# The last two token groups of an attention and MLP-mixer kernel as the column halves of one Strassen product

## The chip, the cores and the metric

The kernel runs on one core of a Trainium2 chip. A core has TensorE (PE; it multiplies a loaded 128 x 128 weight block with up to 512 columns and adds into PSUM), VectorE (DVE), ScalarE (ACT), GpSimd (POOL) and SyncE (SP, whose queue here only issues DMAs). The engines run side by side and meet at semaphores. The metric is device time in microseconds; the runs shown are of one launch each.

## The reference, cut to what matters

Linear attention over 8 batches, 8 heads, 576 tokens and 64 channels a head, and then an MLP mixer over the attention's result x (8 x 576 x 512):

```python
kv = einsum('bhsd,bhse->bhde', softmax_over_tokens(k), v)
x  = einsum('bhsd,bhde->bhse', softmax_over_channels(q), kv)   # heads side by side: 512 channels
h  = relu(x.T @ w_tok1) @ w_tok2          # tokens mix: 576 -> 256 -> 576
u  = x + h.T
h2 = relu(u @ w_ch1) @ w_ch2              # channels mix: 512 -> 1536 -> 512
return u + h2
```

The last two products are most of the work, and the change is there. Below they are ch1 and ch2.

## The kernel before

*Numbers.* The matrix products of the mixer take each float32 operand as a high and a low part of a type that TensorE reads in one pass (F32R), and form three of the four part products: high x high, low x high, high x low. So "one product" of 128 x 128 blocks is always three matmuls. `split` (L128) makes the parts: ACT casts the high one, DVE subtracts it for the low one.

*Units and groups.* The first part of the kernel treats 32 units, a batch and a pair of heads each (`load_unit`, `softmax_k`, `softmax_q`, and the stages in `pe_stages`, L685). A unit's last stage, `stage_u` (L440), writes u transposed (channels in partitions, tokens in columns) into `uT[g]`, high and low. The 4608 tokens are cut into nine groups of 512, counted g = 0 to 8; three buffers hold u for them in turn. The hidden 1536 channels are twelve blocks f of 128, the weights of ch1 and ch2 stay in SBUF as such blocks (`c1_row`, `c2_row`).

*Groups 0 to 2* run ch1 plainly (`ch1`, L472): 12 matmuls of 512 columns for each f into a bank of `ps_h`, then relu and the low part. ch2 (L634) takes such an f and adds 4 x 3 matmuls of 512 columns into four banks of `ps_o`, which `out_end` (L646) adds to u and writes.

*Groups 3 to 8* run ch1 by Strassen's scheme in Winograd's form: 2 x 2 blocks, seven products in place of eight. The 2 x 2 blocks are two f (a pair p = f // 2) by two halves of the 512 input channels, and the two halves of the group's 512 columns. `pair_a` (L599) forms the products P1, P6, P5 and P7, `pair_b` (L615) P2, P3 and P4; each `product` (L580) is 6 matmuls of 256 columns. The DVE adds at L607, L611, L612, L620 and L624 join them into both f's hidden values, and L629 and L630 make relu and the low part for ch2, which stays plain. The sums of data that the products need come from `data_sums` (L568) over the row sums u = high + low (`row_sum`, L562, on POOL or DVE).

*Where the weights come from.* The seven weight operands of a pair (blocks, and sums of blocks) are stored to DRAM once: `keep_blocks` (L495) and `keep_sums` (L503), six pairs each, at steps around the start of group 2. `load_product` (L542) loads one operand of 256 KB at a time into a ring of eight slots, one after each product used. All these DMAs are in SP's queue, in order. The sums pass through the two `stg` buffers, which also hold the row sums of even groups (`rows_of`, L551) until their output is written.

*The order.* `steps` (L761) lists (group, f); n0 = 24 is the step at which group 2 begins, and each later group has 12 steps. `put(at, fn)` hangs unit work, stored sums, row sums and data sums on steps or half steps; ch2 runs one f behind ch1 (`pend`). The units of a batch are hung on the steps of earlier groups, the last of them two steps ahead of group 7. The framework then makes each engine's instruction list by simulating the program, the earlier in the program first among what is ready, and puts in the waits. What an engine does is in that fixed order on the chip.

## Time and profile before

| | |
|---|---|
| median of 3 runs | 810.22 us (808.62 to 810.96) |
| the profiled execution's own time | 805.34 us |
| its span, first to last instruction | 803.5 us |
| granted TensorE clock | 1.00 of full speed |
| PE busy | 778.6 us, 5112 matmuls |
| DVE busy | 606.8 us, 1195 instructions |
| ACT busy | 380.2 us, 908 instructions |
| POOL busy | 113.1 us, 88 instructions |
| DMA | 148.09 MB, mean 184 GB/s |

In the profile's rows "L642 PE MATMUL ps_o<-h,c2h 128*128 128x512 f32 x672 | 225.1, 396" reads: line 642 of the kernel, engine, operation, what is written from what, shapes, how many, busy microseconds, and the mean nanoseconds of one. Matmuls overlap each other in the pipeline, so a matmul's 396 ns is not its share of the time: that is the distance from one start to the next. Behind the second bar stands the time for which the engine had been idle, and what ended that. "c" is a pair's hidden values, "th" and "tl" are the data sums' parts, "ring" the weight operands, "h" the operand of ch2. Groups 7 and 8 have no unit work beside them.

### The profile page before, as it was taken

Reading aid. Unit: us, or ns where it says so; the run is one execution under the profiler, and the core shown is the slowest. Engines: PE = TensorE matmul, PEld = TensorE weight load, DVE = VectorE, ACT = ScalarE, POOL = GpSimd, SP = SyncE. Lnnn points to the kernel's source line nnn. Section 1 sums busy time; section 2 is a strip of 40 time slices with the busy share of each in tenths; the row PEclk is TensorE's granted clock in tenths of the full one; section 3 lists DMA queues with packets and bytes.
Section 4 is the critical chain, followed back from the end, with each engine's and each line's share of the span. In section 5 each row is a group of like instructions: output and inputs, shape, how many; then the busy total and the mean of one; then the engine's idle time right before and its main releaser. Section 6 shows DMA issues by size and latency. Waiting matters only on the chain.

```text
span 803.5 us, 13913 instructions
## 1 busy us (share of the span) xinstructions
PE 778.6 (97%) x5112; PEld 688.9 (86%) x5112; DVE 606.8 (76%) x1195; ACT 380.2 (47%) x908; POOL 113.1 (14%) x88
## 2 busy tenths in 40 slices
PE   3899999989999999999999999999999999999998
PEld 2688888778888888999999899988999999999996
DVE  7989998999889766987797788887896556436333
ACT  4776433465664555655555455445655531122110
POOL 0000000101211331222112222112112201100000
PEclk9999999999999999999999999999999999999999
DMA  9754842315767742666657666766565446556651
GB/s 302 220 153 153 293 148 93 114 60 190 250 236 259 224 144 66 221 208 197 201 181 244 194 203 175 232 196 195 169 189 184 142 144 206 188 169 204 204 170 52
DMA packets 113922, 148.09 MB, mean 184 GB/s; under 512 B 48832, under 2 KB 60736, under 8 KB 113856
## 3 DMA queue, kind: packets, MB, share of 16 engines
q1 hardware_dynamic: 107520, 135.16, 53.9%
q10 hardware_dynamic: 6336, 12.06, 4.0%
q8 instruction: 40, 0.66, 0.3%
q14 instruction: 26, 0.21, 0.1%
HBM read 123.60 MB, written 23.59 MB: 183 GB/s over the span
## 4 chain that ended last, share of the span: by engine, by line
PE 68%; DVE 13%; issue 9%; DMA 5%; ACT 3%; POOL 2%; SPq 0%; DVEq 0%; POOLq 0%; ACTq 0%
PE ps_o L642 26%; PE ps_h L593 19%; PE ps_h L457 6%; PE ps_h L480 5%; PE ps_h L415 4%; DMA q_t<-in_q 4%; PE ps_h L353 2%; PE ps_o L457 1%; PE ps_h L423 1%; DVE st L322 1%; DVE q_t L323 1%; DVE q_t L401 1%; DVE q_t L336 1%; PE ps_o L415 1%; POOL ql L131 1%
## 5 line engine op out<-in xcount | busy, mean ns | idle before, releaser
L642 PE MATMUL ps_o<-h,c2h 128*128 128x512 f32 x672 | 225.1, 396 | 2.4 <-ACT h L483 2.4
L642 PEld LDWEIGHTS ps_o<-h,c2h 128*128 128x128 f32 x672 | 125.5, 188 | 27.2 <-ACT h L483 3.3
L642 PE MATMUL ps_o<-h,c2l 128*128 128x512 f32 x336 | 131.1, 393 | 0.0
L593 PE MATMUL ps_h<-th,ring 128*128 128x256 f32 x576 | 107.1, 283 | 0.7 <-DVE c L624 0.7
L593 PEld LDWEIGHTS ps_h<-th,ring 128*128 128x128 f32 x576 | 89.7, 191 | 0.9 <-DVE c L624 0.9
L593 PE MATMUL ps_h<-uh,ring 128*128 128x256 f32 x432 | 81.7, 282 | 0.0
L593 PE MATMUL ps_h<-tl,ring 128*128 128x256 f32 x288 | 81.4, 283 | 0.0
L593 PEld LDWEIGHTS ps_h<-uh,ring 128*128 128x128 f32 x432 | 70.4, 190 | 4.0 <-issue 0.4
L401 ACT COPY q_t<-cv_s 32x160 f32<-32x160 f32 (+1 forms) x232 | 71.8, 310 | 3.2 <-DVE cv_s L391 0.3
L314 POOL TENSOR_TENSOR k_t<-k_t,dg 128x640 f32<-128x640 f32 x24 | 41.2, 1718 | 222.9 <-ACT dg L313 214.8
L642 PEld LDWEIGHTS ps_o<-h,c2l 128*128 128x128 f32 x336 | 63.4, 189 | 10.4
L131 POOL TENSOR_TENSOR ql<-q_t,qh 128x640 fp32r<-128x640 f32 x24 | 39.4, 1642 | 178.6 <-DMA kt_t<-in_kt 100.9
L593 PE MATMUL ps_h<-ul,ring 128*128 128x256 f32 x216 | 61.0, 282 | 0.0
L629 ACT ACTIVATE h<-c 128x512 fp32r<-128x512 f32 x48 | 28.8, 624 | 60.0 <-DVE c L624 60.0
L480 PE MATMUL ps_h<-uh,c1l 128*128 128x512 f32 x144 | 56.2, 390 | 0.0
L480 PE MATMUL ps_h<-ul,c1h 128*128 128x512 f32 x144 | 56.2, 390 | 0.0
L480 PE MATMUL ps_h<-uh,c1h 128*128 128x512 f32 x144 | 56.1, 392 | 0.0
L593 PEld LDWEIGHTS ps_h<-tl,ring 128*128 128x128 f32 x288 | 55.2, 192 | 0.0
L332 ACT ACTIVATE q_t<-q_t 128x640 f32<-128x640 f32 x32 | 23.6, 739 | 51.1 <-DVE q_t L323 37.5
L464 ACT CAST uh<-ps_h 128x320 fp32r<-128x320 f32 (+4 forms) x76 | 24.7, 335 | 45.9 <-PE ps_h L457 34.3
L322 DVE TENSOR_REDUCE st<-q_t 128x10 f32<-128x640 f32 x32 | 26.2, 818 | 23.7 <-DMA q_t<-in_q 23.4
L593 PEld LDWEIGHTS ps_h<-ul,ring 128*128 128x128 f32 x216 | 41.0, 190 | 0.1
(196 smaller groups left out, 1758.4 us busy)
## 6 DMA issues: line engine op xcount, KB each, us to landing
ring<-w SPq DMA_DIRECT2D x252, 256.0 KB, 3.3
kt_t<-in_kt SPq DMA_DIRECT2D x32, 320.0 KB, 3.3
q_t<-in_q SPq DMA_DIRECT2D x32, 320.0 KB, 3.4
v_t<-in_v SPq DMA_DIRECT2D x32, 320.0 KB, 4.4
stg_w<-in_w SPq DMA_DIRECT2D x18, 512.0 KB, 6.2
k_t<-in_k SPq DMA_DIRECT2D x24, 320.0 KB, 4.8
w<-stg SPq DMA_DIRECT2D x12, 512.0 KB, 3.9
stg<-in_w SPq DMA_DIRECT2D x10, 512.0 KB, 5.1
```

Of the source, the lines that this page charges most:

```text
L131: lo_eng.tensor_tensor(lo, src, f32(hi), op=ALU.subtract)
L314: nc.gpsimd.tensor_tensor(kx, kx, dg.unsqueeze(1).broadcast_to([P, C1, P]), op=ALU.subtract)
L322: nc.vector.tensor_reduce(st[:, 0, :], qt, axis=AX.X, op=ALU.max)
L332: nc.scalar.activation(qc, qc, AF.Exp)
L401: eng(qx[ys, 0:n, xs], turned[xs, 0:n, ys])
L415: nc.tensor.matmul(y[:, 0:TOK], a, w, start=(i == 0), stop=(i == len(mm) - 1))
L457: nc.tensor.matmul(t[:, 0:N], a, w, start=(i == 0), stop=(i == len(mm) - 1))
L464: nc.scalar.copy(uh, src).ins,
L480: nc.tensor.matmul(t, a[:, n, :], w, start=(i == 0), stop=(i == 3 * NJ - 1))
L593: nc.tensor.matmul(t[:, cols], a, b[:, n], start=(i == 0), stop=(i == 5))
L629: nc.scalar.activation(hh, c[:, r], AF.Relu)
L642: m = nc.tensor.matmul(o, a[:, cs], w, start=(first and i == 0), stop=(last and i == 2))
```

## The change

Groups 7 and 8 (GA and GB) leave the step loop, and `both_groups` does them after it, together.

ch1: the two column halves of the 2 x 2 blocks are now group 7 and group 8, so each of the seven products of a pair is 6 matmuls of 512 columns for both groups. The data sums for that are made by `wide_sums` and `wide_split` on the last steps of group 6, from group 7's row sums and, for group 8, sums of its own in tiles of the finished units (`wide_rows`, on POOL). Their parts go into T, where group 6 has used its own, and into the buffer of u that group 6 leaves. The first pair takes its products in another order (`FIRST`), so that the operands that are made last are used last.

ch2: it is done by the same scheme. The 2 x 2 blocks are the two halves of a pair's f in the rows, the two halves of the 512 output channels, and the two groups as columns. Seven products over six pairs, each 6 matmuls of 512 columns; a product of all pairs is summed in two PSUM banks, then joined to the outputs by adds on DVE, ACT and POOL. The weight operands are stored to DRAM by `keep_out` (blocks) and `keep_out_sums` (sums), six times, at the steps in `KEEP`: two in group 2 and four in group 5. The hidden values of all pairs stay in SBUF; `operand` makes the parts of one data operand at a time, up to twelve ahead, and has POOL form the differences that later operands need.

The ring has eight slots as before up to group 6, and six for the joint part. The pools of the main part are closed ahead of it (`main_pools`), and its tiles take their place.

```diff
+    KEEP = (5.5, 7.5, 37, 38.5, 40, 41.5)
+    AHEAD = 12
...
-    scratch_w = {}
+    scratch_w, scratch_v = {}, {}
...
+    def keep_out(p):
+        scratch_v[p] = dpool.tile([P, 7, 2, 2 * P], F32, name=f"v{p}")
+        with behind(loaded):
+            for x, (w0, w1) in enumerate(zip(c2_row(2 * p), c2_row(2 * p + 1))):
+                nc.sync.dma_start(scratch_v[p][:, P1, x, :], f32(w0[:, 0 : 2 * P]))
+                nc.sync.dma_start(scratch_v[p][:, P2 : P4 + 1, x, :], f32(w1).rearrange("p (k m) -> p k m", k=2))
+    def keep_out_sums(p):
+        hi = stg.tile([P, CW, 2], U32, name="stg").rearrange("p n w -> p (n w)").bitcast(F32R)
+        lo = stg.tile([P, CW, 2], U32, name="stg").rearrange("p n w -> p (n w)").bitcast(F32R)
+        a = f32(hi).rearrange("p (f m) -> p f m", f=2)
+        (wh, wl), i = c2[2 * p]
+        nc.gpsimd.tensor_tensor(a, f32(wh[:, i : i + 2]), f32(wl[:, i : i + 2]), op=ALU.add)
+        s = f32(lo).rearrange("p (k m) -> p k m", k=4)
+        (a11, a21), (a12, a22) = ([a[:, f, x * 2 * P : (x + 1) * 2 * P] for x in range(2)] for f in range(2))
+        nc.vector.tensor_tensor(s[:, 0], a21, a22, op=ALU.add)
+        nc.vector.tensor_tensor(s[:, 1], s[:, 0], a11, op=ALU.subtract)
+        nc.vector.tensor_tensor(s[:, 2], a11, a21, op=ALU.subtract)
+        nc.vector.tensor_tensor(s[:, 3], a12, s[:, 1], op=ALU.subtract)
+        split(hi, lo, f32(lo), nc.vector)
+        for x, w in enumerate((hi, lo)):
+            nc.sync.dma_start(scratch_v[p][:, P5 : P3 + 1, x, :], f32(w).rearrange("p (k m) -> p k m", k=4))
...
     def stage_pair_pools(f0):
...
-            pool = ctx.enter_context(tc.tile_pool(name="pairs_b", bufs=1, reuse_waits="tile"))
+            pool = main_pools.enter_context(tc.tile_pool(name="pairs_b", bufs=1, reuse_waits="tile"))
...
-    loads = [(p, e) for g in range(G_S, NG) for p in range(NP) for e in (P1, P6, P5, P7, P2, P3, P4)]
-    asked = [0]
+    TURN = (P1, P6, P5, P7, P2, P3, P4)
+    FIRST = (P1, P5, P2, P3, P6, P7, P4)
+    GA, GB = NG - 2, NG - 1
+    turn_of = [FIRST] + [TURN] * (NP - 1)
+    loads = [(scratch_w, p, e) for g in range(G_S, GA) for p in range(NP) for e in TURN]
+    n_main = len(loads)
+    loads += [(scratch_w, p, e) for p in range(NP) for e in turn_of[p]]
+    loads += [(scratch_v, p, e) for e in TURN for p in range(NP)]
+    slot_of = [i % 8 if i < n_main else (i - n_main) % 6 for i in range(len(loads))]
+    after, to_load, last_in = {}, [], {}
+    for i, x in enumerate(slot_of):
+        (after.setdefault(last_in[x], []) if x in last_in else to_load).append(i)
+        last_in[x] = i
+    def load_at_place(i):
+        where, p, e = loads[i]
+        nc.sync.dma_start(f32(ring[slot_of[i]].rearrange("p n m -> p (n m)")), where[p][:, e].rearrange("p x m -> p (x m)"))
     def load_product():
-        i = asked[0]
-        if i < len(loads):
-            p, e = loads[i]
-            nc.sync.dma_start(f32(ring[i % 8].rearrange("p n m -> p (n m)")), scratch_w[p][:, e].rearrange("p x m -> p (x m)"))
-            asked[0] += 1
+        load_at_place(to_load.pop(0))
+    at_product, at_h = [0], [0]
+    def next_weights():
+        w = ring[slot_of[at_product[0]]]
+        at_product[0] += 1
+        return w
+    def weights_used():
+        for i in after.get(at_product[0] - 1, ()):
+            load_at_place(i)
     rows = {}
...
-    at_product, at_h = [0], [0]
     def product(g, e, t, cols):
-        w = ring[at_product[0] % 8]
-        at_product[0] += 1
+        w = next_weights()
...
-        load_product()
+        weights_used()
...
+    def wide_rows(n):
+        t = ld.tile([P, C1 * P], F32, name="q_t" if n < 2 else "k_t", bufs=2)[:, 0:CW]
+        uh, ul = (x[:, n, :] for x in uT[GB])
+        nc.gpsimd.tensor_tensor(t, f32(uh), f32(ul), op=ALU.add)
+        beside.append(t)
+    def wide_T(i, k):
+        if i < 2:
+            return [x[:, 2 * i + k] for x in T]
+        return [x[:, 2 * (i - 2) + k, :] for x in uT[GA - 1]]
+    def wide_sums(i, k):
+        r = rows_of(GA)
+        b11, b21, b12, b22 = r[0][:, k, :], r[1][:, k, :], beside[k], beside[2 + k]
+        if i == 0:
+            first_diff.append(tf[k])
+            nc.vector.tensor_tensor(tf[k], b12, b11, op=ALU.subtract)
+        elif i == 1:
+            wide_sum.append(cv.tile([P, C1 * P], U32, name="cv_s").bitcast(F32)[:, 0:CW])
+            nc.vector.tensor_tensor(wide_sum[k], b22, first_diff[k], op=ALU.subtract)
+        elif i == 2:
+            nc.vector.tensor_tensor(b12, b22, b12, op=ALU.subtract)
+        else:
+            b21_of[k] = wide_sum[k]
+            nc.vector.tensor_tensor(wide_sum[k], b21, wide_sum[k], op=ALU.subtract)
+    def wide_split(i, k):
+        src = (first_diff[k:], wide_sum[k:], beside[k:], [b21_of.get(k)])[i][0]
+        split(*wide_T(i, k), src, nc.vector)
+    def six(w, pieces_h, pieces_l, outs, first, last):
+        for n in range(2):
+            o = outs[n % len(outs)]
+            one = len(outs) == 1
+            for i, (a, b) in enumerate(((w[:, n], pieces_h[n]), (w[:, 2 + n], pieces_h[n]), (w[:, n], pieces_l[n]))):
+                nc.tensor.matmul(o, a, b, start=first and i == 0 and (n == 0 or not one), stop=last and i == 2 and (n == 1 or not one))
+    def bank():
+        i = banks[0]
+        o = i >= 4 and i // 4 % 2
+        return (ps_o if o else ps_h).tile([P, CW], F32, name="ps_o" if o else "ps_h")
+    def both_groups():
+        pool = ctx.enter_context(tc.tile_pool(name="both", bufs=1, reuse_waits="tile"))
+        places = [tuple(pool.tile([P, CW], F32R, name=f"x{i}{x}") for x in "hl") for i in range(4)]
+        h = [pool.tile([P, 4, CW], F32, name=f"hb{p}") for p in range(NP)]
+        t1 = [pool.tile([P, CW], F32, name=f"tb{p}") for p in range(NP)]
+        places += [tuple(pool.tile([P, CW], F32R, name=f"x{i}{x}") for x in "hl") for i in range(4, 7)]
+        places += [(T[0][:, i], T[1][:, i]) for i in range(4)]
+        places += [(x[0][:, n, :], x[1][:, n, :]) for x in slots for n in range(NJ)]
+        vec, pl = nc.vector.tensor_tensor, nc.gpsimd.tensor_tensor
+        steps2 = [(e, c) for e in TURN for c in range(NP)]
+        made = [0]
+        def operand():
+            i = made[0]
+            if i == len(steps2):
+                return
+            e, c = steps2[i]
+            made[0] += 1
+            src = {P1: h[c][:, 0], P5: h[c][:, 0], P6: t1[c], P7: h[c][:, 1], P2: h[c][:, 2], P3: h[c][:, 3], P4: t1[c]}[e]
+            split(*places[i % len(places)], src, nc.vector)
+            if e == P1:
+                pl(h[c][:, 0], h[c][:, 1], h[c][:, 0], op=ALU.subtract)
+                pl(t1[c], h[c][:, 3], h[c][:, 0], op=ALU.subtract)
+                pl(h[c][:, 1], h[c][:, 3], h[c][:, 1], op=ALU.subtract)
+            if e == P6:
+                pl(t1[c], h[c][:, 2], t1[c], op=ALU.subtract)
+        for p in range(NP):
+            c11, c12, c21, c22 = (h[p][:, i] for i in range(4))
+            y, done = {}, set()
...
+            for e in turn_of[p]:
+                o = bank()
+                w = next_weights()
+                k = {P1: (GA, 0), P2: (GA, 2), P3: (GB, 2)}
+                if e in k:
+                    g, n0 = k[e]
+                    th, tl = ([x[:, n0 + n, :] for n in range(2)] for x in uT[g])
+                else:
+                    i = {P5: 0, P6: 1, P7: 2, P4: 3}[e]
+                    th, tl = zip(*(wide_T(i, n) for n in range(2)))
+                six(w, th, tl, [o], True, True)
+                weights_used()
+                y[e] = o
+                if can("c", P1):
+                    nc.scalar.copy(c11, o)
...
+            operand()
+            if p == 1:
+                for n in range(NJ):
+                    row_sum(GB, n, nc.gpsimd)
+        ra, rb = rows_of(GA), rows_of(GB)
+        sums = tf
+        for e in TURN:
+            last = e == P4
+            y = [bank() for _ in range(2)]
+            ws = []
+            for c in range(NP):
+                for _ in range(2):
+                    if made[0] < at_product[0] - n_main - 7 * NP + AHEAD:
+                        operand()
+                w = next_weights()
+                bh, bl = places[(at_product[0] - 1 - n_main - 7 * NP) % len(places)]
+                if last:
+                    ws.append((w, bh, bl))
+                    continue
+                six(w, [bh] * 2, [bl] * 2, y, c == 0, c == NP - 1)
+                weights_used()
+            for m in range(2):
+                r11, r21, r12, r22, t, o = ra[0][:, m], ra[1][:, m], rb[0][:, m], rb[1][:, m], sums[m], y[m]
+                if last:
+                    for c, (w, bh, bl) in enumerate(ws):
+                        for i, (a, b) in enumerate(((w[:, m], bh), (w[:, 2 + m], bh), (w[:, m], bl))):
+                            nc.tensor.matmul(o, a, b, start=c == 0 and i == 0, stop=c == NP - 1 and i == 2)
+                    for x, eng in ((slice(0, HW), nc.scalar), (slice(HW, CW), nc.sync)):
+                        vec(r21[:, x], o[:, x], r21[:, x], op=add)
+                        eng.dma_start(out[GA, 2 + m][:, x], r21[:, x])
+                elif e == P1:
+                    nc.scalar.copy(t, o)
+                    pl(r11, r11, t, op=add)
+                elif e == P6:
+                    vec(t, o, t, op=add)
+                    pl(r12, r12, t, op=add)
+                elif e == P5:
+                    vec(r12, o, r12, op=add)
+                    vec(r22, o, r22, op=add)
+                elif e == P7:
+                    vec(t, o, t, op=add)
+                    pl(r22, r22, t, op=add)
+                    nc.scalar.dma_start(out[GB, 2 + m], r22)
+                    pl(r21, r21, t, op=add)
+                elif e == P2:
+                    vec(r11, o, r11, op=add)
+                    nc.scalar.dma_start(out[GA, m], r11)
+                else:
+                    vec(r12, o, r12, op=add)
+                    nc.scalar.dma_start(out[GB, m], r12)
...
-    steps += [(g, f) for g in range(2, NG) for f in range(NF)]
+    steps += [(g, f) for g in range(2, GA) for f in range(NF)]
...
-    for g in range(2, NG):
+    for g in range(2, GA):
...
-            last_n = g < NG - 1 and n == NJ - 1
-            put(at - 2 if g < NG - 1 and n > 1 else at - 5, lambda g=g, n=n, last_n=last_n: row_sum(g, n, nc.vector if last_n else nc.gpsimd))
+            last_n = n == NJ - 1
+            put(at - 2 if n > 1 else at - 5, lambda g=g, n=n, last_n=last_n: row_sum(g, n, nc.vector if last_n else nc.gpsimd))
...
+    at = n0 + (GA - 2) * NF
+    for n in range(NJ):
+        x = at - 5 if n < 2 else at - 4 if n < 3 else at - 2
+        put(x, lambda n=n: row_sum(GA, n, nc.vector if n == NJ - 1 else nc.gpsimd))
+        put(x, lambda n=n: wide_rows(n))
+    put(at - 2, lambda: [wide_sums(0, k) for k in range(2)])
+    put(at - 1.5, lambda: [wide_split(0, k) for k in range(2)])
+    put(at - 1.5, lambda: [wide_sums(1, k) for k in range(2)])
+    put(at - 1.5, lambda: wide_split(1, 0))
+    put(at - 0.5, lambda: wide_split(1, 1))
+    put(at - 0.5, lambda: [wide_sums(2, k) for k in range(2)])
+    put(at - 0.5, lambda: [wide_split(2, k) for k in range(2)])
+    put(at - 0.5, lambda: [wide_sums(3, k) for k in range(2)])
+    put(at - 0.5, lambda: [wide_split(3, k) for k in range(2)])
+    for p, x in enumerate(KEEP):
+        put(n0 + x, lambda p=p: keep_out(p))
+        put(n0 + x + 0.5, lambda p=p: keep_out_sums(p))
     put(n0 + 8, lambda: stage_pair_pools(0))
...
-    now = pend.pop(0)
-    ch2(*now[1:])
-    ch2(*pend[0][1:], in_turn=True)
-    out_end(*pend[0][:2], True)
+    for now in pend:
+        ch2(*now[1:])
+    out_end(*pend[-1][:2], True)
+    main_pools.close()
+    both_groups()
```

More of the change, by code (lines that the diff above doesn't have):

```diff
@@ L107, in attn_mixer_kernel @@
     c2 = {}
+    main_pools = ctx.enter_context(ExitStack())
     def c2_rows(f0, f1):
-        late = ctx.enter_context(tc.tile_pool(name=f"late{f0}", bufs=1))
+        late = main_pools.enter_context(tc.tile_pool(name=f"late{f0}", bufs=1))
         h_ = late.tile([P, f1 - f0, DM], F32R, name=f"c2h{f0}")
@@ new lines, in attn_mixer_kernel, with can, relu @@
+    banks = [0]
+    def bank():
+        i = banks[0]
+        banks[0] += 1
+        o = i >= 4 and i // 4 % 2
+        return (ps_o if o else ps_h).tile([P, CW], F32, name="ps_o" if o else "ps_h")
+    add = ALU.add
+    def both_groups():
[26 more added lines that the diff above has]
+            y, done = {}, set()
+            def can(name, *needs):
+                ok = name not in done and all(x in y or x in done for x in needs)
+                if ok:
+                    done.add(name)
+                return ok
+            def relu(c):
+                nc.scalar.activation(c, c, AF.Relu)
+            for e in turn_of[p]:
[13 more added lines that the diff above has]
+                    nc.scalar.copy(c11, o)
+                if can("u2", P6, "c"):
+                    vec(c22, y[P6], c11, op=add)
+                if can("12", P5, "u2"):
+                    vec(c12, y[P5], c22, op=add)
+                if can("u3", P7, "u2"):
+                    vec(c21, y[P7], c22, op=add)
+                if can("11", P2, "u2"):
+                    vec(c11, y[P2], c11, op=add)
+                    relu(c11)
+                if can("22", P5, "u3", "12"):
+                    vec(c22, y[P5], c21, op=add)
+                    relu(c22)
+                if can("12+", P3, "12"):
+                    vec(c12, y[P3], c12, op=add)
+                    relu(c12)
+                if can("21+", P4, "u3", "22"):
+                    vec(c21, y[P4], c21, op=add)
+                    relu(c21)
+            operand()
[48 more added lines that the diff above has]
+                    nc.scalar.dma_start(out[GB, m], r12)
@@ L750, in attn_mixer_kernel @@
     del v_ring[1:], kv_ring[1:]
-    ld = ctx.enter_context(tc.tile_pool(name="ld", bufs=2))
-    wk = ctx.enter_context(tc.tile_pool(name="wk", bufs=1))
+    ld = main_pools.enter_context(tc.tile_pool(name="ld", bufs=2))
+    wk = main_pools.enter_context(tc.tile_pool(name="wk", bufs=1))
     c2_rows(F_HEAD, F_MORE)
```

2 lines of the change are left out of this document (added).

## The prediction

> **What bounds the kernel now.** I read the page first (who is busy, and when), then the waits of TensorE (does it ever wait?), then the chain of waits (at what pace does it run where the change sits?), then the stages around the added work.
>
> ```profile
> span 803.5 us, 13913 instructions
> PE 778.6 (97%) x5112; PEld 688.9 (86%) x5112; DVE 606.8 (76%) x1195; ACT 380.2 (47%) x908; POOL 113.1 (14%) x88
> DVE  7989998999889766987797788887896556436333
> ```
>
> PE is busy 97% of the span, but its ends are modelled, so that alone proves little. DVE's row has two halves that matter here: 8s and 9s while the token units are prepared, and 3 to 6 in the last quarter, where the last two groups run. All waits of TensorE in the whole span:
>
> ```profile
> PE ps_o L302 <- ACT kt_t L299: 6.8, 2, 5.8
> PE ps_o L379 <- issue: 5.5, 1, 5.5
> PE ps_o L642 <- ACT h L483: 2.4, 2, 1.3
> PE ps_o L423 <- ACT ys L417: 1.9, 1, 1.9
> PE ps_h L457 <- ACT qth L130: 1.8, 1, 1.8
> PE ps_h L302 <- ACT kt_t L299: 1.6, 1, 1.6
> PE ps_h L593 <- DVE c L624: 0.7, 1, 0.7
> ```
>
> They sum to 20.7 us, and the pair products of ch1 (L593) wait once, for 0.7 us. So TensorE sets the end. The chain of waits (columns: start, duration, what), from the start of group 7, groups counted from 0 to 8, gives its pace:
>
> ```profile
> 667.87 2.87 PE ps_h L593 x24
> 670.74 2.75 PE ps_o L642 x12
> 673.49 2.15 PE ps_h L593 x18
> 675.64 2.75 PE ps_o L642 x12
> ...
> 730.99 2.87 PE ps_h L593 x24
> ...
> 791.37 6.16 PE ps_o L642 x27
> ```
>
> Group 7 begins at 667.87 (24 matmuls of 256 columns, then 12 of ch2 with 512), group 8 at 730.99: 63.12 us, with no piece of another engine between. A 256-column matmul costs (2.87+2.15)/42 = 119.5 ns, a 512-column one 2.75/12 = 229.2 ns. A pair takes 42 x 0.1195 + 24 x 0.2292 = 10.52 us, and six are 63.1: the pace explains the whole group.
>
> **The change, part by part.** *ch1 of groups 7 and 8.* Each of the 42 products was 6 matmuls of 256 columns for each group, so 12 x 0.1195 = 1.434 us for both; it becomes 6 of 512, 1.375 us. Gain 42 x 0.059 = 2.5 us. *ch2.* The two groups had 2 x 144 = 288 matmuls of 512; seven products of six pairs of 6 are 252. Gain 36 x 0.2292 = 8.25 us. Together 10.7 us. A second way agrees: ch2 of group 6 (two times 2.75) now comes ahead of everything, so the joint part starts at 667.87 + 5.50 = 673.4 and ends 504 x 0.2292 = 115.5 later, at 788.9. The last matmul now starts at 799.17, so its stream ends at 799.4: 10.5 us later.
>
> The Trainium skill, "TensorE: Matmul & The Clock Gate", Back-to-back issue gap, gives a warm gap of N/2.4 + 2.5 ns, 109.2 for 256 and 215.8 for 512 columns; by it, as an estimate, ch1 would gain 0.6 us, ch2 7.8, together 8.4. The trace's 119.5 and 229.2 disagree with it and decide.
>
> *The end.* What follows the last matmul stays: adds in two halves and two writes, some 4 us.
>
> ```profile
> 797.90 2.45 DVE L657 TENSOR_TENSOR stg<-ps_o,stg 128x256 f32<-128x256 f32 x7
> 798.38 2.37 SPq L658 DMA_DIRECT2D out<-stg  x4
> 799.17 0.39 PE L642 MATMUL ps_o<-h3l,c2h 128*128 128x512 f32 x1
> ```
>
> Only the final product's order differs. It runs all six pairs for one row block first, 3 matmuls each, so the sixth weight block is wanted 15 x 0.229 = 3.44 us after that product starts. Its load can be issued only then, since six ring slots are left and the block before it in that slot is the sixth of the product ahead.
>
> ```profile
> L546 SPq DMA_DIRECT2D ring<-w x55: 319/320/959, 700.2 to 780.2; - x55
> DMA to landing us min/median/max: 2.6/3.0/4.8
> ```
>
> That is a loss of 0 to 1.4 us; I take 0.3. Elsewhere a ring slot is refilled five products, 6.9 us, ahead: hidden behind those products' matmuls.
>
> *DVE, ACT and POOL inside the joint part.*
>
> ```profile
> L611 DVE TENSOR_TENSOR c<-ps_h,c 128x512 f32<-128x512 f32 x36 | 24.7, 687 | 8.5 <-PE ps_h L593 7.6
> L131 DVE TENSOR_TENSOR tl<-tf,th 128x512 fp32r<-128x512 f32 x24 | 16.4, 684 | 2.8 <-ACT th L130 2.4
> L130 ACT CAST th<-tf 128x512 fp32r<-128x512 f32 x24 | 14.9, 620 | 20.3 <-DVE tf L575 12.9 <-PE ps_h L593 7.2
> L629 ACT ACTIVATE h<-c 128x512 fp32r<-128x512 f32 x48 | 28.8, 624 | 60.0 <-DVE c L624 60.0
> L564 POOL TENSOR_TENSOR part<-uh,ul 128x512 f32<-128x512 f32 x9 | 11.7, 1295 | 69.8 <-DVE ul L465 62.2 <-DMA out<-part 7.5
> ```
>
> In ch1 a pair (7 x 1.375 = 9.63 us) needs seven PSUM adds and one split: 5.5 us of DVE; ACT four relus, a copy and a cast, 3.7; POOL three differences, 3.9. In ch2 a product (8.25 us) needs six splits and at most four adds, 6.9 us of DVE. All hidden under the matmuls. The data sums are 16 DVE operations and splits as before, with columns doubled and groups halved. At the seam, ch2 of group 6 loses the pair product that ran ahead of it: its operand needs an add, a relu and two splits, 0.69 + 0.62 + 1.37 = 2.7 us, behind the last product at 667.87 - 2.75 = 665.1, and its low half is wanted by the third matmul at 668.3. Bounds 0 and 0.7 (one more DVE operation ahead); I take 0.3. The same seam holds eight more splits and sums on DVE (some 9 us) before the seventh ch1 product at 673.4 + 8.25: 16 us, enough.
>
> *The stored ch2 blocks and sums.* Six times, POOL adds 1024 columns (2 x 1.295 = 2.6 us), DVE does four 256-column operations and a 1024-column split, ACT a cast (1 us), and SP issues six writes, 14 blocks of 128 KB = 1.79 MB. Two fall in group 2, four in the first half of group 5. The prices are those of the stored ch1 sums:
>
> ```profile
> L512 DVE TENSOR_TENSOR stg<-stg x6: 418/420/424, 197.5 to 272.8; 128x256 f32<-128x256 f32 x6
> L131 DVE TENSOR_TENSOR stg<-stg 128x1024 fp32r<-128x1024 f32 x6 | 7.3, 1220 | 1.6 <-ACT stg L130 1.6
> L130 ACT CAST stg<-stg 128x1024 fp32r<-128x1024 f32 x6 | 6.3, 1052 | 8.2 <-DVE stg L514 8.2
> w<-stg SPq DMA_DIRECT2D x12, 512.0 KB, 3.9
> 240.00:260.00 20.00, 20.00 (x115) 16.60 (x114) 19.30 (x37) 10.31 (x24) 2.84 (x2) 1.00 0.76 263
> 505.00:545.00 40.00, 39.34 (x298) 35.81 (x297) 33.13 (x64) 18.72 (x49) 7.90 (x5) 1.00 0.66 207
> 497.60:584.90 87.30, 86.57 (x630) 78.68 (x630) 70.22 (x143) 47.95 (x125) 17.94 (x12) 1.00 0.64 197
> ```
>
> (Windows: length, then busy time of PE, weight load, DVE, ACT and POOL; clock, DMA share, GB/s.) DVE's part is 4 x 0.42 + 1.22 = 2.9 us, four times 11.6, into 40 us in which it has 40 - 33.1 = 6.9 free. DMA's is 4 x 1.79 = 7.2 MB at 207/0.66 = 314 GB/s, 22.8 us, into 40 x 0.34 = 13.6 free. Neither fits where it is put; both fit the whole of group 5 (17.1 us of DVE free, 31.4 of DMA). So they run late and are caught up on slack: ring loads have eight products of 87.3/42 = 2.08 us, 16.6 us, and the units of group 6 end some way ahead of it. With DVE at 19.3 of 20 us and DMA at 0.76, TensorE lost nothing at 240 to 260. The two in group 2 I put at nothing, hidden under the plain ch1 and ch2 matmuls; uncovered, 2.9 us each. In group 5, bounds are 0 and the 4.7 us of DVE that 40 us can't hold; nearer the row that lost nothing, I take 1.2.
>
> Sum: -10.7 + 0.3 + 0.3 + 1.2 = -8.9 against the profiled 805.34 us: 796.4. The three runs' median, 810.22, lies 4.9 above that execution: 801.3.
>
> **The rivals.**
>
> *A. Group 5 pays.* The stored sums chain POOL, DVE, ACT, DVE and a write over two staging buffers, 2.6 + 1.7 + 1.0 + 1.2 + 3.9 = 10.4 us without a queue, at a cadence of 1.5 steps, 87.3/12 x 1.5 = 10.9 us; the row sums of group 6 want the buffers next. SP's queue holds ring loads behind those writes, and DVE already waits there for late input:
>
> ```profile
> DVE st L322 <- DMA q_t<-in_q: 4.9, 3, 2.0
> ```
>
> If lateness lasts to group 6's products, all 4.7 us of overflow and another 4 x 0.5 of such waits are paid, 5.5 more than I took: 806.8. For it: both engines over full. Against: 240 to 260.
>
> *B. POOL holds DVE.* In the new ch2 start, POOL's differences alternate with DVE's splits, and one overlap shows what that does:
>
> ```profile
> 619.53 1.31 POOL L564 TENSOR_TENSOR part<-uh,ul 128x512 f32<-128x512 f32 x1 [9.71 <-DVE ul L465]
> 620.17 1.29 DVE L131 TENSOR_TENSOR qtl<-q_t,qth 128x576 fp32r<-128x576 f32 x1 [0.71 <-ACT qth L130]
> L131 DVE TENSOR_TENSOR qtl<-q_t,qth x24: 700/758/1620, 173.8 to 639.4; 128x576 fp32r<-128x576 f32 x24
> ```
>
> The split took 1.29 instead of 0.76 us: it ended 0.62 after POOL did. If they alternate strictly, an operand costs 0.68 + 1.30 = 1.98 us against 1.375 a product. Six are in hand, 8.25 us; the next six take 11.9, plus the last pair's three differences, 3.9: 15.8 against a deadline of 15.1, and as much again where DVE's adds fall between, up to 4.6: 805.9. Against: only the first two of seven products carry these differences. The Trainium skill, "SBUF — State Buffer", Who interferes with whom, says just that: a DVE instruction with two SBUF inputs and a GpSimd one that reads SBUF block each other wholly; the overlap above agrees.
>
> *C. Slower: DVE saturates in group 5.* The place is 505 to 545, the mechanism that of B on A's work: each POOL sum holds DVE's two-input operations for its 2.6 us. Then DVE gets 4 x (2.9 + 2.6) = 22.0 us into 6.9, 15.1 us late. It decides if the static order leaves PSUM adds behind that work, so that TensorE pays all of it instead of 1.2: 815.2. Against: 17.1 us are free in the group, and most of TensorE's work there doesn't wait for units.
>
> *D. It doesn't do what it says:* 512-column products meet a limit (weight loads at 86%) and only 36 matmuls are saved, 8.25 of 10.7: 803.8. The pace of L642, at 229 with a weight load each, is already that of the new products, so it is unlikely.
>
> **How the numbers follow.** The forecast, 801.3, with its own range 797.8 to 804.5, has 0.54; A 0.18, B 0.10, C 0.13, D 0.05. A measurement of this kernel tells 0.3%, 2.4 us, from no change. The forecast, B and D are faster; A's 806.8 lies near the bound 807.8, so half of it is the same (0.09). Faster 0.78, same 0.09, slower 0.13. The range runs from 797.5 (nothing lost, and a little for the runs' spread) to 808.5 (A whole, with the same): it leaves out C and some of A.
>
> **What would show it.** Right: matmuls of the joint part at 229 ns and 504 of them from about 673 (later by what group 5 paid), ending near 790; no TensorE wait over 1 us there; the tail unchanged. The seam's price is the wait of ch2 on the last h; the end's is a wait on ring in the last product; group 5's is its length against 87.3 us. Wrong: a group 5 longer by over 5 us (A, or C over 12) with DVE near full, DVE splits of 1.3 us with TensorE waiting on x operands in the new ch2 (B), or matmuls slower than 235 ns (D).

## The result: 805.26 us against 810.19, and the profile after

| | before | after |
|---|---|---|
| median | 810.19 us (808.62 to 810.96, 4 runs) | 805.26 us (804.24 to 806.38, 4 runs) |
| the profiled execution's own time | 805.34 us | 804.50 us |
| ratio of the times | | 0.9942, 95% interval 0.992 to 0.9964 |

The change is worth 4.9 us; the forecast, 801.3, was 4.0 us too low. Two rows of the page of the changed kernel (busy time and instructions of each engine; DVE's busy tenths in 40 slices):

```profile
PE 770.3 (96%) x4824; PEld 669.0 (83%) x4824; DVE 654.6 (82%) x1229; ACT 409.7 (51%) x952; POOL 180.2 (22%) x130
DVE  7989998899879787987798679898998557567971
```

PE has 288 matmuls fewer on record. DVE has 48 us more to do, and not only at the end: slices 26 to 30 (about 500 to 600 us), where group 5 lies, are 8, 9, 8, 9, 9; before they were 8, 8, 7, 8, 9.

**The joint part.** Windows (columns: window, its length, busy time of PE, weight load, DVE, ACT and POOL with instructions, granted clock, DMA share, GB/s): first the kernel before, from the first product of group 7 to the last matmul's end, then the changed one, from the first joint product.

```profile
667.87:799.40 131.53, 131.53 (x816) 118.60 (x815) 59.94 (x108) 20.69 (x41) 5.09 (x4) 1.00 0.54 171
```

```profile
679.40:799.20 119.80, 119.69 (x529) 98.80 (x527) 78.90 (x108) 43.78 (x76) 52.77 (x36) 1.00 0.66 193
```

131.53 - 119.80 = 11.7 us less, with 24 matmuls of group 6's ch2 in both. PE is busy for 119.69 of 119.80 us. The chain of waits of the changed kernel in that part (start, duration, what) says why it is a little more than forecast:

```profile
679.41 4.53 PE ps_h L765 x20
683.94 5.44 PE ps_o L691 x24
...
701.17 5.44 PE ps_o L765 x24
...
790.93 8.17 PE ps_o L879 x36
```

The chain stays on PE from 679 to the end. The pace is 5.44/24 = 226.7 ns a matmul in ch1 and ch2 alike, where the 229.2 of before was taken from runs of 12; and the last product, L879, keeps it (8.17/36 = 226.9), so the sixth ring load cost nothing.

**What was lost ahead of it.** The joint part begins 11.5 us later than group 7 did (679.4 against 667.87), so the profiled executions differ by 0.84 us only. Group by group, by the start of each group's first product as counted in the trace, group 5 takes 93.7 us (87.3 in the profiled execution of before, 88.2 in another one of it), and group 6 up to the joint part 84.9 (82.8 in both). The rest stands at the start of group 3, 331.4 against 328.6 (332.2 in the other execution of before). The two later starts have different reasons. In the other execution of before the granted clock fell twice (last section); in the changed kernel's it never fell, and group 2 itself, from its first ch1 matmul to the first product of group 3, takes 91.3 us against 89.1 and 89.8. Kernel 1 below, without any store, takes 91.4 there, so the stores are not the reason; what it is stays open.

Windows around group 5, before and after:

```profile
500.00:595.00 95.00, 94.27 (x676) 85.50 (x676) 79.14 (x162) 52.93 (x141) 19.19 (x12) 1.00 0.62 193
```

```profile
500.00:595.00 95.00, 89.47 (x641) 80.00 (x640) 85.91 (x162) 51.17 (x127) 27.74 (x15) 1.00 0.81 257
505.00:545.00 40.00, 35.81 (x238) 31.30 (x237) 34.16 (x69) 18.66 (x49) 11.04 (x5) 1.00 0.83 276
```

In the same 95 us TensorE got 35 matmuls fewer done. At 95/676 = 0.14 us each that is 4.9 us. In the 40 us in which the prediction wanted 11.6 us more of DVE, DVE was busy 34.16 instead of 33.13: the work came later, as it said, but TensorE waited meanwhile. The chain of the changed kernel in that stretch shows on what:

```profile
510.48 0.60 DVE stg L711
...
511.11 4.04 DMA out<-stg
...
515.31 2.56 POOL stg L538
...
517.89 0.43 DVE stg L541
518.32 0.34 DVE stg L543
518.65 0.68 DVE qtl L135
...
519.38 2.96 DMA q_t<-in_q
...
522.37 0.82 DVE st L326
523.19 1.13 DVE stg L135
...
526.76 2.02 DVE st L338
...
530.98 0.41 DVE c L669
531.39 1.36 DVE stg L541
...
533.84 0.30 DVE stg L542
534.15 0.60 DVE c L673
```

Read it downward. Group 4's output leaves a staging buffer (out<-stg), then POOL may add into that buffer (L538), then DVE makes the differences (L541, L543). Behind them in DVE's fixed order stands `qtl` of a unit, which has nothing to do with the stored sums; the next unit's q load follows it, then that unit's softmax. The same stretch of the chain before:

```profile
512.58 0.68 DVE qtl L131
...
513.32 4.12 DMA q_t<-in_q
...
517.46 0.83 DVE st L322
...
520.85 0.94 DVE st L334
...
524.10 0.07 DVE c L620
```

Against the start of its group (497.6 and 500.6) `qtl` moved from 15.0 to 18.05 us, 3.1 later. The delay does not stay what the wait for the buffer made it. By the same two starts the next `st` (L322, now L326) is 1.9 us later, as this q load was the shorter one; `st` behind the sums' split (L135 on stg) is 2.9 later; and the PSUM add c (L620, now L669) is 3.9 later, behind an `st` of 2.02 us in place of 0.94. Right ahead of the next PSUM add, c L673, stand differences of the second sum (L541 and L542 the second time). So the wait, the arithmetic of the sums and an operation that ran beside POOL are all in this chain. DVE's wait in the changed kernel, and what TensorE then waits for, from the waits of 500 to 600 (total, times, longest):

```profile
DVE stg L541 <- POOL stg L538: 2.3, 1, 2.3
...
PE ps_h L642 <- DVE c L669: 2.0, 1, 2.0
...
PE ps_h L642 <- DVE c L673: 1.2, 1, 1.2
```

The last two are ch1's pair products, which before waited once for 0.7 us (kernel 1 below: once, 1.3).

### The profile page after: what moved, and what is told of

The parts are those of the page before. It is cut to its first block, busy times and chain, and to the rows that moved or that the text cites. A ratio compares the mean times of both kernels' runs of the same rounds, so it can differ in the third digit from the quotient of the medians.

```text
span 802.7 us, 13549 instructions
## 1 busy us (share of the span) xinstructions
PE 770.3 (96%) x4824; PEld 669.0 (83%) x4824; DVE 654.6 (82%) x1229; ACT 409.7 (51%) x952; POOL 180.2 (22%) x130
## 2 busy tenths in 40 slices
DMA packets 124963, 159.10 MB, mean 198 GB/s; under 512 B 49376, under 2 KB 71520, under 8 KB 124896
## 4 chain that ended last, share of the span: by engine, by line
PE 59%; DVE 22%; issue 7%; DMA 7%; ACT 3%; POOL 1%; SPq 0%; DVEq 0%; POOLq 0%; ACTq 0%
PE ps_o L691 16%; PE ps_h L642 10%; PE ps_h L765 7%; PE ps_o L765 6%; PE ps_h L461 6%; DMA q_t<-in_q 4%; PE ps_h L484 4%; PE ps_h L419 4%; DVE q_t L405 2%; PE ps_h L357 2%; DVE q_t L327 1%; DVE st L337 1%; DVE st L326 1%; DVE st L338 1%; PE ps_o L461 1%
## 5 line engine op out<-in xcount | busy, mean ns | idle before, releaser
L691 PE MATMUL ps_o<-h,c2h 128*128 128x512 f32 x544 | 182.4, 397 | 2.5 <-ACT h L487 2.5
L691 PEld LDWEIGHTS ps_o<-h,c2h 128*128 128x128 f32 x544 | 101.3, 188 | 22.6 <-ACT h L487 3.4
L691 PE MATMUL ps_o<-h,c2l 128*128 128x512 f32 x272 | 105.8, 392 | 0.0
L135 POOL TENSOR_TENSOR ql<-q_t,qh 128x640 fp32r<-128x640 f32 x24 | 40.1, 1669 | 177.5 <-PE ps_o L691 101.0
L642 PE MATMUL ps_h<-th,ring 128*128 128x256 f32 x384 | 71.7, 283 | 1.2 <-DVE c L673 1.2
L642 PEld LDWEIGHTS ps_h<-th,ring 128*128 128x128 f32 x384 | 59.9, 191 | 1.6 <-DVE c L673 1.6
L642 PE MATMUL ps_h<-uh,ring 128*128 128x256 f32 x288 | 54.8, 283 | 2.0 <-DVE c L669 2.0
L642 PE MATMUL ps_h<-tl,ring 128*128 128x256 f32 x192 | 54.3, 283 | 0.0
L642 PEld LDWEIGHTS ps_h<-uh,ring 128*128 128x128 f32 x288 | 46.0, 190 | 4.1 <-DVE c L669 2.2
L468 ACT CAST uh<-ps_h 128x320 fp32r<-128x320 f32 (+4 forms) x76 | 24.5, 335 | 46.1 <-PE ps_h L461 30.5
L326 DVE TENSOR_REDUCE st<-q_t 128x10 f32<-128x640 f32 x32 | 26.2, 817 | 24.2 <-DMA q_t<-in_q 24.1
L405 DVE COPY q_t<-cv_s 32x160 f32<-32x160 f32 (+1 forms) x152 | 37.8, 249 | 4.1 <-POOL ql L135 2.3
L469 DVE TENSOR_TENSOR ul<-ps_h,uh 128x320 fp32r<-128x320 f32 (+4 forms) x76 | 27.2, 369 | 13.1 <-ACT uh L468 12.8
```

The costliest lines, as they stand in the source:

```text
L135: lo_eng.tensor_tensor(lo, src, f32(hi), op=ALU.subtract)
L326: nc.vector.tensor_reduce(st[:, 0, :], qt, axis=AX.X, op=ALU.max)
L405: eng(qx[ys, 0:n, xs], turned[xs, 0:n, ys])
L468: nc.scalar.copy(uh, src).ins,
L469: nc.vector.tensor_tensor(ul, src, f32(uh), op=ALU.subtract).ins,
L642: nc.tensor.matmul(t[:, cols], a, b[:, n], start=(i == 0), stop=(i == 5))
```

## The experiments

The theories: S, the stored ch2 blocks and sums cost what was lost; D, it is DVE's arithmetic for them; H, it is DVE standing at the head of its order for a staging buffer, with other work behind. The forecasts also name O (the new order of units makes it late, not the stores), L (POOL's hold on DVE costs) and W (DVE's own work costs, as in D). Ratios are to the kernel before, with their 95% interval. "Pair" is the seven products of two f; group 5 has six.

**1. No stores.** The joint ch2 loads ch1's stored operands in place of its own.

```diff
-    loads += [(scratch_v, p, e) for e in TURN for p in range(NP)]
+    loads += [(scratch_w, p, e) for e in TURN for p in range(NP)]
-        put(n0 + x, lambda p=p: keep_out(p))
-        put(n0 + x + 0.5, lambda p=p: keep_out_sums(p))
```

> The changed kernel without its six stores of ch2 blocks and sums; the joint ch2 reads the stored operands of ch1 in their place, so its output isn't the reference's, but each load, split and matmul of the joint part is there. In the changed kernel's profile the joint part is 12.0 us shorter than groups 7 and 8 were, and begins 11.3 us later. Theory S (the stores make it late): without them the joint part begins within 2 us of group 7's old start, 667.7 us, and the time falls by 8 to 11 us, to 794 to 797. Rival O (the new order of units, row sums and data sums makes it late, whatever is stored): the time stays at 803 to 806.

797.31 us, 0.9856 [0.984, 0.9872]. That is 11.8 us below the kernel before in the same job (809.06): the joint part's whole gain. The stores cost 805.26 - 797.31 = 8.0 us; by the two ratios, (0.9942 - 0.9856) x 809, 7.0. The joint part begins at 671.9 us, not within 2 us of 667.7 as forecast, but 667.7 is from the early execution of before; the other one has 672.2. Its window:

```profile
500.00:595.00 95.00, 93.49 (x678) 85.18 (x677) 76.87 (x155) 52.32 (x138) 21.33 (x13) 1.00 0.64 195
```

678 matmuls, as before the change, and DVE 9.0 us less busy than with the stores.

**2. The stores in the kernel before.** Its groups 7 and 8 stay as they were; nothing reads what is stored.

```diff
+    for p, x in enumerate(KEEP):
+        put(n0 + x, lambda p=p: keep_out(p))
+        put(n0 + x + 0.5, lambda p=p: keep_out_sums(p))
```

> The kernel before with the six stores added at the same steps; nobody reads what they store. Theory S: the stores cost 8 to 11 us here too, 818 to 821. Rival O: the stores are hidden, 809 to 813.

817.73 us, 1.0115 [1.0096, 1.0134]: 8.7 us for the stores alone, with no joint part, a little under the 818 to 821 forecast. S holds from both sides.

**3. Blocks only.** No sums; the four sum operands are read from ch1's.

```diff
-        put(n0 + x + 0.5, lambda p=p: keep_out_sums(p))
```

> The changed kernel with the stored blocks (4.6 of 10.8 MB) and without the stored sums, that is without their POOL add, DVE operations, ACT cast and writes; the joint ch2 reads stored ch1 sums in their place, so its output isn't the reference's. If the engines and staging buffers of the sums are the cost: 794 to 798, as without any store. If the bytes are the cost: about 43% of the stores' cost remains, 799 to 801.

796.51 us, 0.9851 [0.9831, 0.9872]: as without any store. Window of that kernel:

```profile
500.00:595.00 95.00, 93.30 (x676) 84.67 (x674) 77.30 (x154) 51.33 (x132) 22.52 (x13) 1.00 0.73 226
```

The blocks' bytes raise the DMA share from 0.64 to 0.73 and cost hardly a matmul (676 against 678). It is the sums, with their engines' work, their buffers and their own writes.

**4. Other places.** Four kernels differ only in the steps, two sums of group 5 moved to group 3, the sums of group 5 a step later, four in group 2 and two in group 3, or all six in group 2:

```diff
-    KEEP = (5.5, 7.5, 37, 38.5, 40, 41.5)
+    KEEP = (5.5, 7.5, 14, 17, 37.5, 40.5)     first
+    KEEP = (5.5, 7.5, 38, 39.5, 40.5, 41.5)   second
+    KEEP = (5, 6.5, 8, 9.5, 14.5, 17)         third
+    KEEP = (3, 4.5, 6, 7.5, 9, 10)            fourth
```

> The changed kernel with the four stores of group 5 spread: two at steps 14 and 17 after group 2's start (group 3, where the staging buffers are free), two at 37.5 and 40.5. If crowding in group 5 is the cost, most of the 6.4 us that group 5 grew by comes back and little is paid in group 3: 799 to 802. If each store has a price wherever it lies: 804 to 806.

> The changed kernel with the first of group 5's stored sums a step later (stores at 38, 39.5, 40.5 and 41.5 steps after group 2's start). In the profiles with the sums, with and without POOL's add, DVE stands 2.3 to 2.4 us at the head of its list before the first of them, behind the output of group 4 that has to leave the staging buffer, and the PSUM adds queue behind it. Theory H (that wait is what costs): the wait is gone, the second pair of group 5 falls from 17.3 us to about 14.5, and the time to 801 to 803. Theory D (DVE has no free time that TensorE doesn't need, so each sum is paid wherever it lies in groups 3 to 6): 804 to 806.

> The changed kernel with four stores in group 2 (steps 5, 6.5, 8 and 9.5 after its start) and two in group 3 (14.5 and 17), none in group 5. The two in group 2 cost nothing that the start of group 3 shows. Theory H: group 5 is back at about 88 us and group 3 pays at most 1.7, 798 to 800. Theory D: the same, as group 2 has DVE free and group 5 hasn't, 799 to 801. Rival G (group 2 is no freer, its spare time was used up by two): group 3 begins 3 to 5 us later, 802 to 805.

> The changed kernel with all six stores in group 2 (steps 3, 4.5, 6, 7.5, 9 and 10 after its start). Theories H and D: groups 3 to 6 are as without stores; if group 2's DVE takes 17 us more in its free 27%, 797 to 799, within 2 us of the kernel without stores. Rival G: group 3 begins over 5 us later, 803 or more.

806.45 us, 0.9977 [0.9961, 0.9993]; 805.78, 0.9957 [0.9942, 0.9972]; 805.27, 0.9945 [0.993, 0.996]; 810.34, 1.0014 [1.0004, 1.0025]. None gains. That each sum is paid wherever it lies fits the first and the second; crowding missed, and H and D, which both forecast a gain for the third and fourth, missed those. There G's times fit, but not its place: group 3 begins at 333.7 and 334.3 us, some 2 to 3 us later than in the changed kernel, and the larger loss is in the first pairs of group 3. The second was meant to let the buffer come free first, and did not: DVE waited there as before.

```profile
DVE stg L541 <- POOL stg L538: 3.1, 1, 3.1
```

So it says nothing for or against H, though its time is the one that D gave. The third took the sums out of group 5, and windows over group 3 and group 5 show the cost moving with them:

```profile
328.00:420.00 92.00, 88.05 (x650) 79.58 (x650) 84.20 (x155) 50.60 (x125) 26.24 (x16) 1.00 0.75 235
500.00:595.00 95.00, 93.00 (x681) 83.71 (x680) 76.32 (x155) 49.83 (x128) 20.36 (x12) 1.00 0.64 193
```

Group 5 is whole again (681 matmuls), and group 3 has 650 where the changed kernel has 676: DVE is now 84.2 of 92 us busy there. From 240 to 345 us DVE's waits for a staging buffer behind POOL or a write, which the changed kernel hasn't there, are in the third:

```profile
DVE stg L541 <- POOL stg L538: 1.5, 1, 1.5
```

and in the fourth, where the first pair of group 3 takes 19.1 us instead of 10.6 (some 3.3 us of that is a granted clock of 0.59 from 344 to 352 us):

```profile
DVE stg L541 <- DMA v<-stg: 2.6, 1, 2.6
DVE stg L541 <- POOL stg L538: 2.3, 1, 2.3
```

**5. POOL's add.** On DVE instead (the result stays the same), or left out (sums of the high parts only, so another operand of ch2):

```diff
-        nc.gpsimd.tensor_tensor(a, f32(wh[:, i : i + 2]), f32(wl[:, i : i + 2]), op=ALU.add)
+        nc.vector.tensor_tensor(a, f32(wh[:, i : i + 2]), f32(wl[:, i : i + 2]), op=ALU.add)   first
+        a = f32(wh[:, i : i + 2])                                                              second
```

> The changed kernel with the add of high and low part in the stored sums on DVE in place of POOL. In the changed kernel's profile POOL's 2.4 us adds hold DVE: a 10-column operation of 0.16 us took 2.02 and ended with the POOL add. Theory L (POOL's hold of DVE is the cost of the stored sums): although DVE gets 6 x 1.22 us more work, most of the 8 us comes back, 798 to 801. Theory W (DVE's own work is too much for group 5): it gets worse, 807 to 811.

> The changed kernel without that add: the sums are formed from the high parts alone, so its output isn't the reference's; DVE's four operations, split, cast and all writes stay. Theory L: the time is that without stores, 796 to 799. Theory W: DVE's 2.9 us for each store still cost most of it, 802 to 805.

803.23 us, 0.9928 [0.9908, 0.9947], and 804.92, 0.9951 [0.9933, 0.997]. Both intervals overlap the changed kernel's. L's forecasts (798 to 801, 796 to 799) both missed; W's held for the second (802 to 805) and missed for the first. POOL's hold on DVE is thus not the whole price; a gain of 1 to 2 us is left open. In the second DVE itself now stands for the buffer that group 4's output leaves:

```profile
DVE stg L540 <- DMA out<-stg: 2.4, 1, 2.4
```

**6. No differences and no split on DVE.** ACT copies the low part; what is stored are not the sums.

```diff
-        nc.vector.tensor_tensor(s[:, 0], a21, a22, op=ALU.add)
...
-        split(hi, lo, f32(lo), nc.vector)
+        nc.scalar.copy(lo, f32(hi))
```

> The changed kernel without DVE's part of the stored sums: its four differences and the low part are left out, an ACT copy of the same size stands in the cast's place, so its output isn't the reference's; POOL's add, both staging buffers and all writes stay. Theory D (DVE's 2.9 us a store is what TensorE pays for, about half of it): 797 to 799, as without stores. Rival B (the staging buffers, the writes or POOL's hold are what costs, each alone enough to keep the delay that taking POOL's add away left): 803 to 806.

807.04 us, 0.9978 [0.9963, 0.9994]: above both forecasts, and no gain from 2.9 us less of DVE per sum. But it does not refute D, since ACT took over the standing, and longer; the waits of ACT from 500 to 600:

```profile
ACT stg L539 <- DMA v<-stg: 7.8, 1, 7.8
ACT stg L539 <- POOL stg L538: 2.1, 1, 2.1
```

What DVE's arithmetic saved and what ACT's new waits cost can't be told apart here. In this execution the granted clock also fell twice in the stretch (the number before the DMA share in these windows):

```profile
528.00:532.00 4.00, 3.07 (x15) 2.99 (x16) 2.05 (x5) 3.94 (x10) 2.71 (x2) 0.69 1.12 346
540.00:544.00 4.00, 4.00 (x20) 3.96 (x20) 3.21 (x7) 2.46 (x6) 1.23 (x1) 0.60 1.06 392
```

**7. The add as a reload.** ch2's whole weights are saved to DRAM at the start; SP loads a pair of them into the staging buffer where POOL added. DVE's differences, split and the writes stay, and the result.

```diff
-        nc.gpsimd.tensor_tensor(a, f32(wh[:, i : i + 2]), f32(wl[:, i : i + 2]), op=ALU.add)
+        nc.sync.dma_start(f32(hi), whole_out[p])
```

> The changed kernel with the add taken away by other data: the whole ch2 weights are written to DRAM where they are split, as those of ch1 are, and loaded into the staging buffer where the POOL add was; the result is the reference's. Theory L: 797 to 800, better than the changed kernel by 5 or more, unless the six writes of 512 KB near the kernel's start cost something there (then up to 803). Theory W: 803 to 806.

807.24 us, 0.9983 [0.9968, 0.9998], above both forecasts. The start pays for the saving: group 2 begins at 248.0 us (240.1 in the changed kernel, 242.4 in another run of the one before). Group 5, though, is nearly whole, with four full sums of DVE work in it and more DMA than in any other window of these 95 us shown:

```profile
500.00:595.00 95.00, 93.09 (x680) 83.84 (x679) 81.08 (x167) 51.04 (x126) 17.18 (x11) 1.00 0.86 283
```

No wait of DVE for a staging buffer is named any more (0.6 us ahead of its first difference are put down to nothing that the profile shows); SP stands for it instead:

```profile
SPq L544 <- DMA out<-stg: 3.8, 1, 3.8
```

The two pairs of group 5 in which the first sums fall tell the kernels apart (counted from the trace, first matmul to first matmul):

| kernel | sums in these pairs | their wait for a staging buffer | pairs 2 + 3, us |
|---|---|---|---|
| before, shown at the start | none | none | 30.5 |
| before, again | none | none | 31.3 |
| 1, no stores | none | none | 31.2 |
| 3, blocks only | none | none | 32.0 |
| 4, third and fourth | none | none | 31.7, 31.8 |
| 7, reload | yes | SP 3.8 | 31.0 |
| changed | yes | DVE 2.3 | 35.2 |
| 2, stores in before | yes | DVE 2.8 | 35.2 |
| 4, first | yes | DVE 3.1 | 35.5 |
| 4, second | yes | DVE 3.1 | 35.6 |
| 5, DVE adds | yes | DVE 3.0 | 35.2 |
| 5, no POOL add | yes | DVE 2.4 | 35.1 |
| 6, no DVE | yes | ACT 2.1 and 7.8 | 39.4 |

Clock drops add up to 1.7 us to kernel 2 and the first two of 4, and up to 3.4 to kernel 6; the changed kernel and both of kernel 5 have none there. The loss of some 4 us stands where an engine with other work in its order waits for the buffer, and not where SP does. That speaks for H, but another reading fits as well. Windows of the two pairs, and of the four pairs behind them, in kernel 1, then in the changed kernel, and of the two pairs in kernel 7:

```profile
514.47:545.65 31.18, 29.85 (x228) 26.93 (x227) 23.96 (x43) 13.67 (x37) 8.16 (x5) 1.00 0.68 213
545.65:602.44 56.79, 56.61 (x405) 51.91 (x403) 46.38 (x100) 34.62 (x89) 11.03 (x7) 1.00 0.60 183
```

```profile
514.10:549.28 35.18, 30.99 (x228) 27.21 (x227) 27.92 (x54) 16.43 (x42) 11.78 (x6) 1.00 0.86 281
549.28:609.20 59.92, 57.60 (x405) 51.78 (x403) 57.80 (x109) 34.29 (x87) 16.98 (x11) 1.00 0.72 227
```

```profile
521.41:552.38 30.97, 30.55 (x228) 26.98 (x227) 25.85 (x55) 16.95 (x42) 4.24 (x3) 1.00 0.98 333
```

In the two pairs DVE is idle for 7.2 us without stores and for 7.3 with them: its wait for the buffer took the place of waits for q loads (from 500 to 600, in kernel 1 and in the changed kernel):

```profile
DVE st L326 <- DMA q_t<-in_q: 5.6, 4, 2.7
```

```profile
DVE st L326 <- DMA q_t<-in_q: 0.8, 2, 0.4
```

What grew is its busy time, by 4.0 us, as much as the pairs. In kernel 7 it is busy for 2.1 us less than in the changed kernel, so DVE's work there is not the same; and the reload also moves the later sums: two fall in these pairs, three in kernel 5's second. In the four pairs behind, the changed kernel loses 3.1 us more, and there DVE has 2.1 us left idle of 59.9, against 10.4: a nearly full DVE is the plainer reading there, though in kernel 7 the same four pairs take 60.8 us with 8.9 of DVE idle. Busy time alone does not set the price either: in group 5, kernel 5's second has DVE busy for 77.9 us, the changed kernel for 84.7, and its group is only 1.3 us shorter. Nor does kernel 7 get all back: its last pair of group 5 and first of group 6 take 16.9 and 16.4 us (15.4 and 13.4 without stores; 16.7 and 14.8 in the changed kernel). So S is shown, and that it is the sums; how the price divides between the wait (H), DVE's own work (D) and POOL's hold (L) stays open. A kernel with two more staging buffers, which would take only the wait away, was not tried.

**8. The kernel before, profiled again.**

```diff
(no edit)
```

> The kernel before, unchanged, once more with a profile. The profiled execution shown was 805.34 us against a median of 810; in it group 3 began at 328.6 us, in all profiles since at 331 to 333. If that execution was a quick one in its first 330 us: here group 3 begins at 331 to 333 and the time is 808 to 810. If the change moved the start of group 3: 328 to 329 again.

809.79 us, as forecast for a quick execution at the start. Group 3 begins at 332.2 us, not 328.6, and most of that is a granted clock that fell twice; what it shows stands in the last section.

## Why the prediction was right, and where it was not

*What bounds the kernel, and the products.* Right. TensorE sets the end, and the matmuls saved came off it whole: -10.7 with 0.6 for seam and end was forecast, -11.7 measured. The pace is 226.7 ns, not 229.2: 528 matmuls x 2.5 ns = 1.3 us of the difference. The Trainium skill, "TensorE: Matmul & The Clock Gate", Back-to-back issue gap, gives N/2.4 + 2.5, so 215.8 for 512 columns, as the gap of an isolated warm matmul, and about 131 ns for a stream of them with weight loads. The trace agrees with neither: it shows 226.7 where the chain is nothing but such matmuls with a weight load each. The row was the better base, as the prediction chose.

*The seam and the end* (0.3 each): nothing at either. The window of the joint part leaves 0.11 us of PE idle in all, and L879 runs at the pace of the others.

*The stored ch2 blocks and sums* (1.2 us): this step failed. They cost 7.0 to 8.0 us by kernel 1 and 8.7 by kernel 2; in the profiled executions 178.6 us from the start of group 5 to the joint part against 171.0 both in the second execution of before and in kernel 1, 7.6. The prediction's own sign of being wrong came, too: group 5 is 6.4 us longer, over the 5 it named. The arithmetic was sized right (four differences of 0.42 us and a split of 1.22; the bytes are a little more, 159.10 - 148.09 = 11.0 MB for six stores, 1.84 each where 1.79 was taken), and that it runs later was right, too. But from the second pair of group 5 to the first of group 6 DVE is busy for 85.7 us against 70.3 in kernel 1, 15.4 more, where 11.6 were counted; operations beside POOL's adds became longer, as the `st` of 2.02 us. Of these 15.4, 8.3 went into idle time of DVE, and 7.1 made the stretch longer. Wrong was thus the overlap, "caught up on slack", and where its size was taken from: "nearer the row that lost nothing", the window 240 to 260, where DVE is 19.3 of 20 us busy and TensorE loses nothing. That window says that a busy DVE does not by itself hold TensorE up. It says nothing of a stretch in which the chain of waits runs through DVE. The prediction had the waits of TensorE, which are short in group 5, but did not read the chain there: it runs through DVE's unit work already before the change (`qtl`, `st` and the q load in the rows above), so only about half of DVE's 17.1 idle us was room. Kernel 4's third and fourth variants put sums into group 2, behind that window, and lost there and at the start of group 3.

*The two in group 2 at nothing.* Not contradicted: group 2 takes 91.3 us, against 91.4 without stores.

*The rivals.* A came nearest: it named the chain over the two staging buffers and lateness in DVE's order, though not that DVE itself would stand for a buffer, and nearly its price: 1.2 + 5.5 = 6.7 us against 7.0 to 8.0. Its 806.8 lies nearer to 805.26 than the forecast; it was 1.5 too high since the products gained more than it assumed. B did not come: no wait in the joint part. C's price, 15.1 us late and all of it paid, did not come; its near-full DVE did, behind the third pair of group 5 (57.8 of 59.9 us busy), and POOL's hold on DVE is in the chain, but taking POOL's add away gained nothing that the interval tells from zero (kernel 5, second). D did not come: the pace is 226.7 ns.

*The sum.* 1.6 us too little gain and 5.8 to 6.8 us too little loss make 4.2 to 5.2 us; the miss was 4.0. That the time still lies in the range is in part luck: two errors went opposite ways, and the range reached so high for A's sake, not for the price that the forecast itself gave the stores. Adding the 4.9 us between the profiled execution and the median was needed: the changed kernel's own profiled execution lies 0.8 us under its median, but that of before was an early one.

## What to carry to other kernels

Before you call an engine's idle time room for more work, read the chain of waits in that stretch: where it already runs through that engine, a good part of the added work is paid for, here about half. In a fixed order, ask of each added instruction what it waits for and what stands behind it, and also which waits it only takes the place of: here DVE stood 2.3 us for a buffer and was idle no longer than without the stores. A measured "nothing lost" at a high load holds for the waits of that place, not for the load as such.

## What the runs showed of the hardware

**The granted clock falls in some executions of one program and not in others.** Windows of the same two stretches of the kernel before, first its second profiled execution, then the one shown at the start (the granted clock is the number before the DMA share):

```profile
29.00:35.00 6.00, 5.29 (x36) 4.23 (x36) 6.00 (x15) 4.91 (x12) 0.00 (x0) 0.72 0.57 188
172.00:178.00 6.00, 4.88 (x15) 3.89 (x16) 5.16 (x14) 4.45 (x14) 0.00 (x0) 0.72 0.15 44
```

```profile
29.00:35.00 6.00, 5.05 (x43) 4.02 (x44) 5.72 (x14) 5.20 (x13) 0.00 (x0) 1.00 0.60 205
172.00:178.00 6.00, 6.00 (x30) 5.13 (x29) 5.09 (x14) 3.59 (x11) 0.00 (x0) 1.00 0.19 55
```

A mean of 0.72 over 6 us is 0.28 x 6/0.5 = 3.4 us at half clock, so each drop costs up to 1.7 us; two explain most of the 3.6 us by which group 3 starts later. Each begins right behind a pause of TensorE (the idle time in brackets); here ahead of the first:

```profile
29.71 0.86 PE L423 MATMUL ps_o<-kvf,ys 128*128 128x128 f32 x4 [1.92 <-ACT ys L417]
```

The same pause, 1.91 us, stands in the execution whose clock did not fall.

The Trainium skill, "TensorE: Matmul & The Clock Gate", Part 1: The HAM clock gate, states a half rate after an idle window of some 3.4 us whose start is not tied to the program. The length of the drop, the rate and the change between executions agree; the pause ahead of the drops, 1.92 and 1.95 us, is shorter. The drops are not all of the spread: in the jobs of the experiments 70 runs of the kernel before lie between 806.8 and 811.7 us, and the 14 of them with a clock of 1.000 still have a median of 808.8. The 805.34 shown at the start lies under all of them.

**An operation of DVE beside a POOL add takes longer, and taking the add away gained nothing to be seen.** In the chain after, `st` L338, 128 x 10 elements, took 2.02 us from 526.76, ending with a POOL add of the sums; the same operation took 0.94 in the chain before, and 0.17 in the median of its 32. The Trainium skill, "SBUF — State Buffer", Who interferes with whom, describes such a lock, and the row agrees; leaving POOL's add out (kernel 5, second) gained nothing that the interval tells from zero.
